# A linear-attention and two-layer MLP kernel on one core: denominators spread by a one-row matmul, float64 weights turned by a scaled copy

## The chip, the core and the metric

The kernel runs on one core of a Trainium2 chip, as one program. The metric is the device time in microseconds. Three runs of the kernel before took 970.0, 970.24 and 970.7 us; the median is 970.24 us.

## The reference, cut to what matters

```python
# q, k, v: (4, 8, 576, 64) float32, w_phi: (64, 128) float32, MLP weights: (512, 2048) and (2048, 512), handed over as float64
def phi(x):
    proj = np.einsum('bhsd,df->bhsf', x, w_phi)
    proj = proj - np.max(np.abs(proj), axis=-1, keepdims=True)
    return np.concatenate([np.exp(proj), np.exp(-proj)], axis=-1)
q_p, k_p = (phi(q), phi(k))
kv = np.einsum('bhsf,bhsd->bhfd', k_p, v)
z = np.sum(k_p, axis=2)
num = np.einsum('bhsf,bhfd->bhsd', q_p, kv)
den = np.einsum('bhsf,bhf->bhs', q_p, z)[..., None] + 1e-06
attn_out = num / den                      # (4, 8, 576, 64) -> x: (2304, 512)

h = x @ w_in;  g = h * (1.0 / (1.0 + np.exp(-h)));  x = g @ w_out              # first layer
h = np.maximum(x @ moe2_w_in, 0.0);  out = (h * h) @ moe2_w_out                 # second layer
```

## The kernel before, in words

The work is cut into eight half blocks of 288 tokens (half a batch each) for the attention, and into six groups of tokens (288, 288, and four times 432) for the first layer. Heads are taken in pairs, p from 0 to 3. `keys_of` makes for each batch and pair the projected keys (`pk`), their exponentials and the product with the values (`pkv`, copied to `kv`). `queries_of(b, p)` does one pair of half block b: the projected queries (`pq`, copied to `qp`), the peak over the features on GpSimd (`qm`), the subtraction on DVE, two exponentials on ScalarE (`qe`), the matmul `pn` with `kv`, which gives 64 rows of numerators and, in row 64, the denominators of 2 x 288 tokens, and a copy of `pn` to the tile `qn` (`num` in the code). For the first batch (b = 0 and 1) these matmuls are float32; later ones are split in a high and a low part.

The denominators stand in one partition. The kernel before spreads them in four steps: a transfer lays the 576 numbers out as 96x6 (`rr`, L1121), DVE adds 1e-6 and takes the reciprocal (L1124, L1125), a second transfer writes them to memory (`rd`, L1128), a third reads them back into 64 partitions (`qb`, L1131). Then DVE multiplies (`x`, L1147), and the product is split in a high part (ScalarE, L431) and a low part (DVE, L435). In the rows `x<-qn,qb` is the product and `x<-x,x` the low part of the split.

The first layer's chunk c of 16 needs the four pairs of its tokens for `h` (L1185) and the weights of chunk c. `h` goes through tanh (ScalarE), a product (DVE, L1193), and a split (`gh` on ScalarE, `gl` on DVE), and then into `o` (L1224). The order number in h_15 is the chunk.

The weights arrive as float64. `w_conv` builds a float32 from the two 32-bit halves: ScalarE takes the magnitude of the upper half (`mag`, L551), and DVE does four steps (`bits`): a clamp (L557), a double shift (L559), an OR with the top bits of the lower half (L563), and an OR with the sign (L567). One call handles 1024 columns in the first layer (16 calls) and 512 in the second (32 calls). `w_split` then makes the high part and the low part (`w<-wc,w`, L435).

The order of the work is not written out by hand. Each step is an `op` with a key, an engine, a cost and buffers; `Plan.run` goes through time with these costs and, whenever an engine is free, takes the ready step with the lowest key whose buffers are free. The order so found is the program's order on each engine, and each engine follows it strictly. The keys come from the table `KEYS`. PSUM has eight banks, parted into pools; `pq` and `pn` of the first half block, like those of the later ones, come from a pool of two banks (`att`).

Of the kernel before, what the change touches and what calls it, by code (L numbers as in the profile page):

```python
# [3 lines left out]

# [5 lines left out]
F32 = mybir.dt.float32  # L10
# [9 lines left out]
NP = H // 2  # L20
# [32 lines left out]
def float_of(bits):
    return struct.unpack("<f", struct.pack("<I", bits))[0]

MIN_HI = float_of(896 << 20)
MAX_HI = float_of((1151 << 20) - 1)

# [227 lines left out]
def dma(kb):  # L288
    return kb
# [11 lines left out]
}  # L301
# [3 lines left out]
def attention_then_two_mlps(ctx, tc, kT, qT, v, w_phi, w1, w2, out):  # L305
# [223 lines left out]
    def w_conv(layer, c, parts, key):  # L529

        n = f"{layer}_{c}_{parts[0]}"
        cols = 512 * len(parts)
        u = plan.unit()
        if layer == 0:
            raw = w_tile("bits", c)
            f = Buf("raw", lambda: rp.tile([128, cols], F32, tag="raw", name="wc" + n), None)
        else:
            raw = Buf("raw", lambda: rp.tile([128, 2 * cols], I32, tag="raw", name="wr" + n), None)  # L540
            f = Buf("c", lambda: cp.tile([128, cols], F32, tag="c", name="wc" + n), None)

        def load():
            src = (w1, w2)[layer][c, :, parts[0] * 512:parts[0] * 512 + cols].bitcast(I32)
            nc.sync.dma_start(out=get(raw), in_=src)

        def halves():
            return get(raw).rearrange("p (n two) -> p n two", two=2)

        def mag():  # L550
            nc.scalar.activation(out=get(f), in_=halves()[:, :, 1].bitcast(F32), func=AF.Abs)  # L551

        def bits(i):
            t, b = get(f), get(f).bitcast(I32)
            lo, hi = halves()[:, :, 0], halves()[:, :, 1]
            if i == 0:
                nc.vector.tensor_scalar(out=t, in0=t, scalar1=MIN_HI, scalar2=MAX_HI, op0=ALU.max, op1=ALU.min)  # L557
            elif i == 1:
                nc.vector.tensor_scalar(  # L559
                    out=b, in0=b, scalar1=5, scalar2=2, op0=ALU.logical_shift_left, op1=ALU.logical_shift_right  # L560
                )
            elif i == 2:
                nc.vector.scalar_tensor_tensor(  # L563
                    out=b, in0=lo, scalar=29, in1=b, op0=ALU.logical_shift_right, op1=ALU.bitwise_or
                )
            else:
                nc.vector.scalar_tensor_tensor(  # L567
                    out=b, in0=hi, scalar=-(1 << 30), in1=b, op0=ALU.bitwise_and, op1=ALU.bitwise_or
                )

        k = ("wf", layer, c, parts[0])
        hold = max([0] + [NC * i + x for i in range(NL) for x in range(NC) if key_of(i, x) <= key - 6]) if layer else 0
        r = [(("c", 0, hold // NC, hold % NC), "h")] if layer else []
        ld = op(key - P["wl"], "SP", dma(cols), load, r=r, w=[(k, 0)], bufs=[raw])
        if layer == 0:
            ld.behind = splits.get(c - NWR)
        op(key, "ACT", act(cols), mag, r=[(k, 0)], w=[(k, 1)], bufs=[raw, f], unit=u)
# [424 lines left out]
    def queries_of(b, p, key, lo_engine="DVE"):  # L1002
# [113 lines left out]
        rb = slot("qb" + n, u, (D, 2, HB))

        rr = Buf("rr", lambda: sp.tile([RP, RN], F32, tag="rr", name="rr" + n), None)

        def spread():  # L1120
            nc.sync.dma_start(out=get(rr), in_=get(num)[D:, :, :].rearrange("p a t -> p (a t)"))  # L1121

        def recip():
            nc.vector.tensor_scalar_add(get(rr), get(rr), 1e-6)  # L1124
            nc.vector.reciprocal(out=get(rr), in_=get(rr))  # L1125

        def r_store():
            nc.sync.dma_start(out=rd[b * NP + p].rearrange("(p f) -> p f", p=RP), in_=get(rr))  # L1128

        def r_load():  # L1130
            nc.sync.dma_start(  # L1131
                out=get(rb).rearrange("p a t -> p (a t)"), in_=rd[b * NP + p].partition_broadcast(D)
            )

        op(key, "SP", dma(3), spread, r=[(Q, "num", 0), (Q, "num", 1)], w=[(Q, "r0")], bufs=[num, rr], unit=u)
        op(key, "DVE", 300, recip, r=[(Q, "r0")], w=[(Q, "r1")], bufs=[rr])
        op(key, "SP", dma(3), r_store, r=[(Q, "r1")], w=[(Q, "r2")], bufs=[rr])
        op(key, "SP", dma(144), r_load, r=[(Q, "r2")], w=[(Q, "r3")], bufs=[rb], unit=u)
        late = b > 0 and p % 2
        x = Buf(  # L1140
            "xy" if late else "xx",
            lambda: (late_pool() if late else sp).tile([128, HB], F32, tag="xx", bufs=1 if late else 2, name="x" + n), None
        )

        def mul():
            for a in range(2):
                nc.vector.tensor_tensor(  # L1147
                    out=get(x)[a * D:(a + 1) * D], in0=get(num)[:D, a, :], in1=get(rb)[:, a, :], op=ALU.mult
                )

        op(key, "DVE", 2 * dve(HB), mul, r=[(Q, "r3"), (Q, "num", 0), (Q, "num", 1)], w=[(Q, "x")],
           bufs=[num, x, rb], unit=u)
        for i, s0, s1 in pieces(b):
            xb = x_buf(i)
            here, there = slice(s0 - b * HB, s1 - b * HB), slice(s0 - STARTS[i], s1 - STARTS[i])

            def x_hi(xb=xb, here=here, there=there):
                hi_act(get(xb)[0][:, p, there], get(x)[:, here])

            def x_lo(xb=xb, here=here, there=there):  # L1160
                lo_on("DVE", get(xb)[1][:, p, there], get(x)[:, here], get(xb)[0][:, p, there])

            op(key, "ACT", act(s1 - s0), x_hi, r=[(Q, "x")], w=[("xh", i, b, p)], bufs=[x, xb])
            op(key, "DVE", dve(s1 - s0), x_lo, r=[(Q, "x"), ("xh", i, b, p)], w=[("xl", i, b, p)], bufs=[x, xb])
# [523 lines left out]
```

## Time and profile before

| | us |
|---|---|
| median of three runs | 970.24 |
| profiled execution | 969.21 |
| span of the profiled execution, first to last instruction | 967.4 |
| TensorE busy | 946.9 |
| VectorE busy | 752.2 |
| ScalarE busy | 613.8 |
| GpSimd busy | 155.8 |

The busy times are of the whole span. An engine that is not the bottleneck may stand idle without cost, and a share of the whole says little about a stage; the stages stand in the rows below. PE is TensorE, DVE is VectorE, ACT is ScalarE, POOL is GpSimd, SP is the engine that issues most transfers. A float32 matmul of the first batch shows as two records.

### The profile page before, as it was taken

The numbers are of one execution on the slowest core, as the hardware profiler recorded it, in microseconds if no ns is written. First come the engines' busy times: TensorE is split into PE (matmuls) and PEld (weight loads), VectorE is DVE, ScalarE is ACT, GpSimd is POOL, SyncE is SP. The second block draws the span as 40 slices with busy tenths as digits, with TensorE's granted clock in tenths as the row PEclk, the third lists the DMA queues.
The fourth block names the chain that finished last, engine by engine and source line by source line (L and its number), as shares of the span: only waits on it lengthen the run. The fifth ranks groups of instructions, "written<-read, shape, count | busy, mean of one in ns | idle before, by whom it ended". The sixth has DMA issues, their size and how long they took to land.

```text
span 967.4 us, 17669 instructions
## 1 busy us (share of the span) xinstructions
PE 946.9 (98%) x6464; PEld 915.0 (95%) x6464; DVE 752.2 (78%) x1362; ACT 613.8 (63%) x1418; POOL 155.8 (16%) x132
## 2 busy tenths in 40 slices
PE   9969999999999999999999999999999999999998
PEld 7749989999999999999999999999999999999998
DVE  6999999777559867889766867885647899898851
ACT  6868877778678887876434444766657765444421
POOL 3140012200042000321000313233110440000000
PEclk9989999999999999999999999999999999999999
DMA  8538645354224654567567575665437774444431
GB/s 315 200 139 324 209 153 172 124 186 136 84 88 132 209 168 136 169 179 253 186 211 263 191 263 166 217 225 217 147 115 237 219 233 121 142 153 134 139 93 51
DMA packets 82322, 171.76 MB, mean 178 GB/s; under 512 B 14906, under 2 KB 39610, under 8 KB 75578
## 3 DMA queue, kind: packets, MB, share of 16 engines
q1 hardware_dynamic: 82234, 170.63, 53.2%
q8 instruction: 51, 0.84, 0.4%
q14 instruction: 37, 0.30, 0.1%
HBM read 123.77 MB, written 46.75 MB: 176 GB/s over the span
## 4 chain that ended last, share of the span: by engine, by line
PE 89%; DVE 7%; ACT 2%; issue 1%; DMA 0%; DVEq 0%; ACTq 0%
PE o L1224 20%; PE h L1185 20%; PE y L1513 17%; PE pb L1341 7%; PE pc L1341 5%; PE pa L1341 5%; PE pn L1106 4%; PE pkv L907 3%; PE pk L845 3%; PE pkv L953 2%; DVE w L435 2%; DVE wc L567 1%; PE pq L1043 1%; PE pq L1044 1%; DVE x L1147 1%
## 5 line engine op out<-in xcount | busy, mean ns | idle before, releaser
L1185 PE MATMUL h<-x,w 128*128 128x432 f32 (+1 forms) x1152 | 217.2, 338 | 2.3 <-DVE x L435 1.7
L1224 PE MATMUL o<-gh,w 128*128 128x432 f32 (+1 forms) x768 | 215.7, 339 | 0.0
L1185 PEld LDWEIGHTS h<-x,w 128*128 128x128 f32 x1152 | 196.8, 188 | 9.4 <-DVE x L435 2.1
L1224 PEld LDWEIGHTS o<-gh,w 128*128 128x128 f32 x768 | 139.8, 188 | 3.9
L1224 PE MATMUL o<-gl,w 128*128 128x432 f32 (+1 forms) x384 | 130.2, 339 | 1.6 <-DVE gl L435 1.4
L1054 POOL PARTITION_ALL_REDUCE qm<-qp x32 | 76.0, 2392 | 261.4 <-ACT qp L1047 236.0
L1189 ACT ACTIVATE a<-h 128x432 f32<-128x432 f32 (+1 forms) x96 | 47.8, 499 | 75.4 <-PE h L1185 75.1
L678 POOL TENSOR_TENSOR ws<-ws 128x256 f32<-128x256 f32 x56 | 52.9, 946 | 198.9 <-DVE wl L435 85.3
L1193 DVE SCALAR_TENSOR_TENSOR a<-a,h 128x432 f32<-128x432 f32 (+1 forms) x96 | 52.7, 550 | 39.2 <-ACT a L1189 38.7
L1224 PEld LDWEIGHTS o<-gl,w 128*128 128x128 f32 x384 | 72.2, 188 | 4.2 <-DVE gl L435 2.5
L435 DVE TENSOR_TENSOR gl<-a,gh 128x432 fp32r<-128x432 f32 (+1 forms) x96 | 57.5, 600 | 14.7 <-ACT gh L431 13.7
L431 ACT CAST gh<-a 128x432 fp32r<-128x432 f32 (+1 forms) x96 | 50.0, 522 | 20.8 <-DVE a L1193 20.3
L1072 ACT ACTIVATE qe<-qp 128x576 f32<-128x576 f32 x64 | 42.1, 683 | 9.3 <-DVE qp L1060 8.4
L879 ACT ACTIVATE ke<-pk,mx 112x128 f32<-112x128 f32 (+1 forms) x160 | 44.5, 376 | 1.0 <-DVE x L1147 0.5
L1513 PE MATMUL y<-yb,w 128*128 128x256 f32 x316 | 44.7, 282 | 0.0
L1106 PE MATMUL pn<-qh,kv 128*65 128x288 f32 x192 | 41.8, 294 | 0.0
L1513 PEld LDWEIGHTS y<-yb,w 128*128 128x128 f32 x316 | 40.7, 189 | 0.0
L435 DVE TENSOR_TENSOR qo<-qe,qh 128x576 fp32r<-128x576 f32 x48 | 36.8, 773 | 4.6 <-ACT qh L431 3.9
L850 DVE TENSOR_REDUCE mx<-pk 112x4 f32<-112x512 f32 (+1 forms) x48 | 28.5, 598 | 14.4 <-PE pk L845 14.1
L953 PEld LDWEIGHTS pkv<-v,kp 112*128 112x128 f32 (+1 forms) x320 | 36.7, 192 | 0.3
L1356 DVE TENSOR_TENSOR glq<-pb,aq 128x288 f32<-128x288 f32 x32 | 14.6, 455 | 28.7 <-PE pb L1341 28.7
L953 PE MATMUL pkv<-v,kp 112*128 112x128 f32 (+1 forms) x320 | 36.9, 275 | 0.0
(425 smaller groups left out, 2601.5 us busy)
## 6 DMA issues: line engine op xcount, KB each, us to landing
w<-w1d SPq DMA_DIRECT2D x30, 1024.0 KB, 5.4
wbits<-w SPq DMA_DIRECT2D x16, 1024.0 KB, 5.9
wr<-w SPq DMA_DIRECT2D x32, 512.0 KB, 5.2
fold<-gd SPq DMA_DIRECT2D x32, 512.0 KB, 3.7
w2d<-wc SPq DMA_DIRECT2D x32, 256.0 KB, 4.1
qr<-qT SPq DMA_DIRECT2D x56, 144.0 KB, 3.4
ws<-w2d SPq DMA_DIRECT2D x28, 256.0 KB, 5.7
w1d<-w SPq DMA_DIRECT2D x6, 1024.0 KB, 4.5
```

Source lines behind the costliest of these rows:

```text
L431: nc.scalar.copy(out=dst, in_=src)
L435: e.tensor_tensor(out=dst, in0=src, in1=hi.bitcast(F32), op=ALU.subtract)
L678: nc.gpsimd.tensor_tensor(out=get(f)[:, o], in0=get(f)[:, a], in1=get(f)[:, b], op=how)
L953: nc.tensor.matmul(get(ps)[:, o:o + 128], get(kps[2 * g + s])[:nt, 2 * i + a], get(vt)[:nt, c:c + 128], start=t == 0 and a == 0 and s == 0 ...
L1054: nc.gpsimd.partition_all_reduce(get(mx), get(pr).rearrange("p a t -> p (a t)"), 128, bass.bass_isa.ReduceOp.absmax)
L1106: nc.tensor.matmul(get(ps)[:D1, :HB], w, get(e)[:, t], start=x == 0, stop=x == len(ops) - 1)
L1185: nc.tensor.matmul(get(ps)[:, :cols], a, x[:, cc, :cols], start=k == 0, stop=k == 3 * ND - 1)
L1189: nc.scalar.activation(out=get(gb)[0][:, :cols], in_=get(ps)[:, :cols], func=AF.Tanh, scale=0.5)
L1193: nc.vector.scalar_tensor_tensor(out=a, in0=a, scalar=1.0, in1=get(ps)[:, :cols], op0=ALU.add, op1=ALU.mult)
L1224: nc.tensor.matmul(get(acc)[:, :cols], a, g[:, :cols], start=c == 0 and x == 0, stop=c == NC - 1 and x == 2)
L1341: nc.tensor.matmul(get(ps)[:, :HB], ws[a][:, f], x[y][:, cc], start=first and k == 0, stop=k == 5, skip_group_check=True,)
L1513: nc.tensor.matmul(get(acc)[:, d * 256:d * 256 + half], get(ws[a][0])[:, ws[a][1], s], both(y)[:, j], start=q == 0 and d == 0 and x == 0, ...
```

## The change

There are two parts, and a new table of keys.

The first: for the first half block (b = 0, four head pairs) DVE adds 1e-6 and takes the reciprocal in place, on the one partition of `qn` that holds the denominators (1x576). Two matmuls with one row of ones as the weights (`ones_row`, set once) spread them over 64 partitions of two PSUM banks (`pr`), and DVE multiplies the numerators with these, one half after the other. The three transfers stay for the later half blocks.

The second: the upper half of a float64 is multiplied on ScalarE with 2^-112, which lowers the exponent as wanted, and the clamp goes. DVE has three steps in place of four: a shift to the left by three with a mask, and the two ORs.

The table of keys has eight other numbers, so that the planner orders many steps in another way.

```diff
-    "k0s": 13.54, "q0s": 16.25, "q0": 5.97, "w0": 42.81, "ws": 4.4, "we": 0.61, "Q1": -4.1, "A1": -0.68,
+    "k0s": 13.54, "q0s": 16.5, "q0": 5.97, "w0": 43.52, "ws": 4.4, "we": 0.61, "Q1": -4.1, "A1": -0.68,
...
+    ones_row = const.tile([D1, D], F32, name="ones_row")
...
+        nc.vector.memset(ones_row[D:], 1.0)
...
         def mag():
-            nc.scalar.activation(out=get(f), in_=halves()[:, :, 1].bitcast(F32), func=AF.Abs)
+            nc.scalar.activation(out=get(f), in_=halves()[:, :, 1].bitcast(F32), func=AF.Copy, scale=2.0 ** -112)
 
         def bits(i):
-            t, b = get(f), get(f).bitcast(I32)
-            lo, hi = halves()[:, :, 0], halves()[:, :, 1]
+            b, lo, hi = get(f).bitcast(I32), halves()[:, :, 0], halves()[:, :, 1]
             if i == 0:
-                nc.vector.tensor_scalar(out=t, in0=t, scalar1=MIN_HI, scalar2=MAX_HI, op0=ALU.max, op1=ALU.min)
+                nc.vector.tensor_scalar(
+                    out=b, in0=b, scalar1=3, scalar2=0x7FFFFFFF, op0=ALU.logical_shift_left, op1=ALU.bitwise_and
+                )
             elif i == 1:
-                nc.vector.tensor_scalar(
-                    out=b, in0=b, scalar1=5, scalar2=2, op0=ALU.logical_shift_left, op1=ALU.logical_shift_right
-                )
-            elif i == 2:
                 nc.vector.scalar_tensor_tensor(
                     out=b, in0=lo, scalar=29, in1=b, op0=ALU.logical_shift_right, op1=ALU.bitwise_or
                 )
             else:
                 nc.vector.scalar_tensor_tensor(
-                    out=b, in0=hi, scalar=-(1 << 30), in1=b, op0=ALU.bitwise_and, op1=ALU.bitwise_or
+                    out=b, in0=hi, scalar=-(1 << 31), in1=b, op0=ALU.bitwise_and, op1=ALU.bitwise_or
                 )
...
-        for i in range(4):
-            op(key, "DVE", dve(cols, i < 2), lambda i=i: bits(i), r=[(k, 1 + i)], w=[(k, 2 + i) if i < 3 else k],
+        for i in range(3):
+            op(key, "DVE", dve(cols, i < 1), lambda i=i: bits(i), r=[(k, 1 + i)], w=[(k, 2 + i) if i < 2 else k],
...
+        row = b < 1
+        if row:
+            def invert():
+                nc.vector.tensor_scalar_add(get(num)[D:], get(num)[D:], 1e-6)
+                nc.vector.reciprocal(out=get(num)[D:], in_=get(num)[D:])
+
+            op(key, "DVE", 1050, invert, r=[(Q, "num", 0), (Q, "num", 1)], w=[(Q, "r2")], bufs=[num], unit=u)
+            over = [bank(f"pr{n}_{a}", u) for a in range(2)]
+            for a in range(2):
+                def copies(a=a):
+                    nc.tensor.matmul(get(over[a])[:D, :HB], ones_row[D:], get(num)[D:, a, :], start=True, stop=True)
...
+        def mul(a):
+            by = get(over[a])[:D, :HB] if row else get(rb)[:, a, :]
+            nc.vector.tensor_tensor(out=get(x)[a * D:(a + 1) * D], in0=get(num)[:D, a, :], in1=by, op=ALU.mult)
```

DVE's order at the place where the first denominators are ready, before: `mx` belongs to the keys of pair 3, `wc` and `w` to the weights of chunks 0 and 1.

```order
L557 TENSOR_SCALAR wc_1_0_371<-wc_1_0_371 128x1024
L559 TENSOR_SCALAR wc_1_0_371<-wc_1_0_371 128x1024
L850 TENSOR_REDUCE mx_3_0_390<-pk_3_0_373 112x4
L435 TENSOR_TENSOR w_0_0_380<-wc_0_0_332,w_0_0_380 128x2x512
L563 SCALAR_TENSOR_TENSOR wc_1_0_371<-wbits_0_162,wc_1_0_371 128x1024
L850 TENSOR_REDUCE mx_3_1_415<-pk_3_1_400 112x4
L850 TENSOR_REDUCE mx_3_2_426<-pk_3_2_409 128x2
L567 SCALAR_TENSOR_TENSOR wc_1_0_371<-wbits_0_162,wc_1_0_371 128x1024
```

The same place after (the line numbers are those of the changed kernel): `qn_0` and `qn_1` are the pairs' tiles, `pr` the spread reciprocals, `x_0` and `x_1` the products.

```order
L549 TENSOR_SCALAR wc_1_0_372<-wc_1_0_372 128x1024
L1109 TENSOR_SCALAR qn_0_377<-qn_0_377 1x576
L1110 RECIPROCAL qn_0_377<-qn_0_377 1x576
L426 TENSOR_TENSOR w_0_0_381<-wc_0_0_334,w_0_0_381 128x2x512
L840 TENSOR_REDUCE mx_3_0_402<-pk_3_0_374 112x4
L1109 TENSOR_SCALAR qn_1_396<-qn_1_396 1x576
L1110 RECIPROCAL qn_1_396<-qn_1_396 1x576
L1151 TENSOR_TENSOR x_0_415<-qn_0_377,pr_0_0_406 64x288
L840 TENSOR_REDUCE mx_3_1_420<-pk_3_1_398 112x4
L1151 TENSOR_TENSOR x_0_415<-qn_0_377,pr_0_1_413 64x288
L1151 TENSOR_TENSOR x_1_432<-qn_1_396,pr_1_0_427 64x288
```

One weight step has gone, and two additions, two reciprocals and four products stand in front of the weights of chunk 1.

PE's order in front of the first h, before: `pn` of the second half block's last pairs, then `h` of chunks 0 to 2 and the keys `pk` of the next batch.

```order
L1106 MATMUL pn_3_0_694<-qe_3_0_676,kv_3_537 65x288
L1106 MATMUL pn_3_0_694<-qe_3_1_684,kv_3_537 65x288
L1106 MATMUL pn_3_1_707<-qe_3_0_676,kv_3_537 65x288
L1106 MATMUL pn_3_1_707<-qe_3_1_684,kv_3_537 65x288
L1185 MATMUL h_0_735<-x_648,w_0_0_380 128x288 x12
L1185 MATMUL h_1_759<-x_648,w_1_0_437 128x288 x12
L845 MATMUL pk_3_0_788<-wbl,kr_3_725 112x256 x2
```

The same place after.

```order
L1096 MATMUL pn_0_1_638<-qe_0_0_612,kv_0_309 65x288
L1096 MATMUL pn_0_1_638<-qe_0_1_616,kv_0_309 65x288
L1030 MATMUL pq_3_0_651<-qr_3_215,wbl 128x288
L1030 MATMUL pq_3_1_656<-qr_3_215,wbl 128x288
L1194 MATMUL h_0_663<-x_446,w_0_0_381 128x288 x12
L835 MATMUL pk_3_0_686<-wbl,kr_3_630 112x256 x2
L1096 MATMUL pn_1_0_695<-qe_1_0_676,kv_1_364 65x288
L1096 MATMUL pn_1_0_695<-qe_1_1_680,kv_1_364 65x288
L1194 MATMUL h_1_705<-x_446,w_1_0_494 128x288 x12
```

Before, all four pairs' `pn` of the second half block stand ahead of the first `h`; after, only pair 0's do, and those of pairs 1 to 3 follow between the first chunks.

## Rows read from the trace of the kernel before

**Rows 1.** The page, busy time of each engine: us (share of the span) xinstructions.

```profile
PE 946.9 (98%) x6464; PEld 915.0 (95%) x6464; DVE 752.2 (78%) x1362; ACT 613.8 (63%) x1418; POOL 155.8 (16%) x132
```

**Rows 2.** Stages: us, PE, PEld, DVE, ACT, POOL busy (instructions), PEclk, DMA share, GB/s.

```profile
48.00:72.00 24.00, 16.04 (x61) 9.55 (x60) 22.84 (x36) 15.90 (x33) 10.73 (x4) 0.86 0.39 136
72.00:96.00 24.00, 23.75 (x174) 22.79 (x172) 23.79 (x44) 21.17 (x63) 0.24 (x2) 1.00 0.90 327
...
300.00:400.00 100.00, 100.00 (x616) 96.44 (x615) 81.12 (x142) 79.77 (x209) 11.96 (x9) 1.00 0.53 171
```

**Rows 3.** What PE waited for, 0 to 150 us: us, times, longest.

```profile
PE pn L1106 <- ACT qe L1072: 5.8, 1, 5.8
...
PE h L1185 <- DVE x L435: 1.7, 2, 0.8
PE o L1224 <- DVE gl L435: 1.4, 2, 1.1
```

**Rows 4.** PE in order of time: start, us, what, idle before it.

```profile
27.46 2.10 PE L1106 MATMUL pn<-qe,kv 128*65 128x288 f32 x8
29.40 1.46 PE L845 MATMUL pk<-wbl,kr 128*112 128x256 f32 x6
...
31.67 9.10 PE L953 MATMUL pkv<-v,kp 112*128 112x128 f32 x80
...
55.67 10.83 PE L1106 MATMUL pn<-qe,kv 128*65 128x288 f32 x32 [5.81 <-ACT qe L1072]
...
70.49 2.12 PE L1185 MATMUL h<-x,w 128*128 128x288 f32 x14 [0.85 <-DVE x L435]
...
144.47 3.42 PE L1185 MATMUL h<-x,w 128*128 128x288 f32 x24 [0.17 <-DVE w L435]
```

**Rows 5.** DVE in order of time: start, us, what.

```profile
42.68 0.68 DVE L557 TENSOR_SCALAR wc<-wc 128x1024 f32<-128x1024 f32 x1
43.28 1.21 DVE L563 SCALAR_TENSOR_TENSOR wc<-wbits,wc 128x1024 int32<-128x1024 int32 x1
44.42 0.68 DVE L559 TENSOR_SCALAR wc<-wc 128x1024 int32<-128x1024 int32 x1
...
47.90 1.21 DVE L435 TENSOR_TENSOR w<-wc,w 128x1024 fp32r<-128x1024 f32 x1
49.03 1.21 DVE L567 SCALAR_TENSOR_TENSOR wc<-wbits,wc 128x1024 int32<-128x1024 int32 x1
...
61.91 0.75 DVE L1060 TENSOR_TENSOR qp<-qp,qm 128x576 f32<-128x576 f32 x1
62.58 1.22 DVE L563 SCALAR_TENSOR_TENSOR wc<-wbits,wc 128x1024 int32<-128x1024 int32 x1
...
69.98 0.45 DVE L435 TENSOR_TENSOR x<-x,x 128x288 fp32r<-128x288 f32 x1
70.35 1.22 DVE L563 SCALAR_TENSOR_TENSOR wc<-wbits,wc 128x1024 int32<-128x1024 int32 x1
...
145.38 1.60 DVE L435 TENSOR_TENSOR qo<-qe,qh 128x576 fp32r<-128x576 f32 x2
```

**Rows 6.** The tile rr on DVE: durations in ns, min/median/max, first and last start.

```profile
L1124 DVE TENSOR_SCALAR rr<-rr x32: 125/161/1285, 40.9 to 474.1; 96x6 f32<-96x6 f32 x32
L1125 DVE RECIPROCAL rr<-rr x32: 186/186/189, 41.1 to 474.3; 96x6 f32<-96x6 f32 x32
```

**Rows 7.** DVE's groups by line and shape: busy us, mean ns, idle before.

```profile
L435 DVE TENSOR_TENSOR ql<-qr,ql 64x576 fp32r<-64x576 f32 x24 | 18.0, 755 | 4.9 <-ACT ql L431 4.3
...
L557 DVE TENSOR_SCALAR wc<-wc 128x512 f32<-128x512 f32 x32 | 14.6, 457 | 3.9 <-ACT wc L551 3.8
...
L856 DVE TENSOR_TENSOR kd<-pk,mx 112x512 f32<-112x512 f32 x6 | 4.1, 687 | 0.1
...
L496 DVE TENSOR_TENSOR wbl_lo<-wbl,wst_hi 64x128 fp32r<-64x128 f32 x2 | 0.6, 279 | 0.0
```

More of the change, by code (lines that the diff above doesn't have):

```diff
@@ L1 @@
 import heapq
-import struct
 from contextlib import ExitStack
@@ L50, in key_of @@
     return NC * STARTS[i] / HB + c * WIDTHS[i] / HB
[L53 to L59, printed above, removed]
 class Op:
@@ L1114, in queries_of @@
             op(key, "ACT", act(HB, True), evac, r=[(Q, "n", a)], w=[(Q, "num", a)], bufs=[ps, num], unit=u)
[L1116 to L1137, printed above, removed]
@@ L1138, in queries_of, with spread, recip, r_store @@
-        op(key, "SP", dma(144), r_load, r=[(Q, "r2")], w=[(Q, "r3")], bufs=[rb], unit=u)
+        row = b < 1
[8 more added lines that the diff above has]
+                    nc.tensor.matmul(get(over[a])[:D, :HB], ones_row[D:], get(num)[D:, a, :], start=True, stop=True)
+                op(key, "PE", 4 * MM, copies, r=[(Q, "r2"), "blank"], w=[(Q, "r3", a)], bufs=[num, over[a]], unit=u)
+        else:
+            rb = slot("qb" + n, u, (D, 2, HB))
+            rr = Buf("rr", lambda: sp.tile([RP, RN], F32, tag="rr", name="rr" + n), None)
+            def spread():
+                nc.sync.dma_start(out=get(rr), in_=get(num)[D:, :, :].rearrange("p a t -> p (a t)"))
+            def recip():
+                nc.vector.tensor_scalar_add(get(rr), get(rr), 1e-6)
+                nc.vector.reciprocal(out=get(rr), in_=get(rr))
+            def r_store():
+                nc.sync.dma_start(out=rd[b * NP + p].rearrange("(p f) -> p f", p=RP), in_=get(rr))
+            def r_load():
+                nc.sync.dma_start(
+                    out=get(rb).rearrange("p a t -> p (a t)"), in_=rd[b * NP + p].partition_broadcast(D)
+                )
+            op(key, "SP", dma(3), spread, r=[(Q, "num", 0), (Q, "num", 1)], w=[(Q, "r0")], bufs=[num, rr], unit=u)
+            op(key, "DVE", 300, recip, r=[(Q, "r0")], w=[(Q, "r1")], bufs=[rr])
+            op(key, "SP", dma(3), r_store, r=[(Q, "r1")], w=[(Q, "r2")], bufs=[rr])
+            op(key, "SP", dma(144), r_load, r=[(Q, "r2")], w=[(Q, "r3")], bufs=[rb], unit=u)
@@ L1143, in queries_of @@
         )
-        def mul():
+        def mul(a):
+            by = get(over[a])[:D, :HB] if row else get(rb)[:, a, :]
+            nc.vector.tensor_tensor(out=get(x)[a * D:(a + 1) * D], in0=get(num)[:D, a, :], in1=by, op=ALU.mult)
+        if row:
             for a in range(2):
[L1147 to L1152, printed above, removed]
+                op(key, "DVE", dve(HB), lambda a=a: mul(a), r=[(Q, "r3", a), (Q, "num", a)], w=[(Q, "x", a)],
+                   bufs=[num, x, over[a]], unit=u)
+            got = [(Q, "x", 0), (Q, "x", 1)]
+        else:
+            op(key, "DVE", 2 * dve(HB), lambda: [mul(a) for a in range(2)],
+               r=[(Q, "r3"), (Q, "num", 0), (Q, "num", 1)], w=[(Q, "x")], bufs=[num, x, rb], unit=u)
+            got = [(Q, "x")]
         for i, s0, s1 in pieces(b):
@@ L1161, in x_lo @@
                 lo_on("DVE", get(xb)[1][:, p, there], get(x)[:, here], get(xb)[0][:, p, there])
-            op(key, "ACT", act(s1 - s0), x_hi, r=[(Q, "x")], w=[("xh", i, b, p)], bufs=[x, xb])
-            op(key, "DVE", dve(s1 - s0), x_lo, r=[(Q, "x"), ("xh", i, b, p)], w=[("xl", i, b, p)], bufs=[x, xb])
+            op(key, "ACT", act(s1 - s0), x_hi, r=got, w=[("xh", i, b, p)], bufs=[x, xb])
+            op(key, "DVE", dve(s1 - s0), x_lo, r=[*got, ("xh", i, b, p)], w=[("xl", i, b, p)], bufs=[x, xb])
     accs = {}
```

4 rows, old and new, of the table KEYS are left out of this document.

## The prediction

> **What bounds the kernel now.** I read the page first, then the stages, then what TensorE waits for, then the two engines' rows in order of time. The page shows TensorE (PE) busy 946.9 of 967.4 us and VectorE (DVE) 752.2 [rows 1]. The stages show where the missing 20 us lie: from 200 us on PE is full (100.00 of 100.00 from 300 to 400, DVE 81.12), but from 48 to 72 us it is busy only 16.04 of 24 and its granted clock falls to 0.86, while DVE is busy 22.84 [rows 2]. So one stage has another limit than the rest: at the start DVE is the bound, later PE is. The list of PE's waits agrees: its longest is 5.8 us in front of pn, and most others end on DVE's x or gl [rows 3]. The rows of that stage show why: PE stands before 55.67, does 16 pn matmuls (32 records, two to a float32 matmul) in 10.83 us, and gets the last part of the first h only at 70.49 [rows 4]. That part waits for DVE's x<-x, which starts at 69.98 and ends at about 70.35 [rows 5]. This last x is the event to follow: the numerators of head pair 3 pass through the adding of 1e-6, the reciprocal, three transfers, the product and the split, all threaded through a full DVE queue.
>
> **The change part by part.** The sum is made against the profiled execution, 969.21 us with a span of 967.4; the median of the runs shown is 970.24, so I add 1.0 at the end.
>
> *DVE up to the last x.* I count the instructions that stand ahead of the last x in DVE's order, before and after, and price them by the distance from one start to the next in a full queue [rows 5]: a tensor_scalar on 1024 columns 0.60 us (42.68 to 43.28), a scalar_tensor_tensor 1.14 (43.28 to 44.42), a split of w 1.13 (47.90 to 49.03), a qp subtraction 0.67 (61.91 to 62.58). Before, 14 such tensor_scalars stand ahead of it, after, 5: -5.4 us. Two scalar_tensor_tensors, two splits and three subtractions move behind it: -2.3, -2.3 and -2.0. Six small pairs on rr go from in front of it: 0.161 and 0.186 us less some overlap, 0.29 a pair, -1.7 [rows 6]. Four tensor_scalars on 1x576 come in. The 96x6 one takes 161 ns and one on 1024 columns 0.68 us [rows 5, 6], so 576 columns take 0.45, less 0.08 of overlap (0.68 long, but the next starts after 0.60): 0.37 each, +1.5. Without the reciprocals this is -12.2 us. The eight half products stay eight; that they read PSUM now costs nothing that I can see, since subtractions that read pk take 687 ns for 512 columns, no more than other rows of that width [rows 7].
>
> *The four reciprocals on one partition.* The trace has reciprocals on 6 columns only: 186 ns [rows 6]. Plain two-input rows take 279 ns at 128 columns and 687 at 512 [rows 7], a slope of 1.06 ns and 143 ns at no columns. Two readings bound the price. If the reciprocal streams like every other row of the trace and has only a longer start, 576 columns take 186 + 570 x 1.06 = 790 ns, less overlap 0.71 us. If all 43 ns above 143 are its six elements, it is 7.2 ns an element and, with the fixed part of a full queue, 4.2 us. I take 0.71, since no other DVE row of this trace streams at more than about 1.06 ns when undisturbed, and a constant of 37 ns explains 186 as well; I keep 4.2 for the range. The Trainium skill (VectorE: DVE Perf Modes, section First, the fixed hardware budget) says that the reciprocal is an iterated divide with a repeat count of eight. Eight passes of 1.04 ns would give an estimate of 4.8 us; no run here shows a long reciprocal, and the 6-column row lies between the two. With 0.71 the four add 2.8: DVE reaches the last x 12.2 - 2.8 = 9.4 us earlier, at 60.9.
>
> *PE up to the first h.* Eight one-row matmuls are new. No row shows one with a single row of weights; a float32 matmul of the same 288 columns takes 0.485 us (27.46 to 29.40 for four) [rows 4], so eight cost 3.9; from below they could cost nothing, if one row were free, but then no streamed column cost anything, so I take 3.9. From 30.4 us to the end of the first h PE then has 40 pkv at 0.223 (80 records in 9.10, less the drain), 30 matmuls at 0.485, one pk and 12 h at 0.13 [rows 4]: 25.5 us. That fits into the 31 us to 61.3, so the 3.9 us lie in what was idle time, and DVE still sets the first h. PE's instructions run in order, so a late reciprocal would hold up pq and pkv behind it; at 0.71 us that is a us or two.
>
> *PE from the first h to the last h of the first half block (h_15).* Before, the first h ends at about 70.9 and h_15 at 147.9 (144.47 plus 3.42) [rows 4]: 77.0 us, nearly all busy, with 1.9 us of waits. After, 12 pn matmuls of the second half block stand behind the first h instead of ahead (5.8 us) and 8 single-pass pq come forward (1.05): 83.9 us. From 61.3 that is 145.2, 2.7 earlier, and the 1.05 is work done ahead of time: 3.7 us in all.
>
> *Does DVE hold that pace?* From the last x to the last split of w before h_15 DVE took 75.0 us (70.35 to 145.38) [rows 5]. After: 7 tensor_scalars fewer (-4.2), the two scalar_tensor_tensors, two splits, two qp and two rr pairs that were moved (+2.3, +2.3, +1.3, +0.6), and two ql more at 0.75 (+1.5) [rows 7]: 78.8, which ends at 139.7, and two h of 1.6 behind it at 142.9. So PE is the limit, with 2.3 us in reserve.
>
> *What costs or gives nothing.* The 32 tensor_scalars removed from the second layer's weights (457 ns each [rows 7]) lie in the stage where PE is full and DVE has a fifth of its time free [rows 2]: zero; were that cover gone, they would be 10 us. The Abs that becomes a scaled copy stays one pass of ScalarE over the same columns: zero either way. Twelve transfers leave SyncE's queue; x no longer waits for them, which is the 9.4 already counted. The other shifts of order fall into full PE time; I allow 1 us either way.
>
> Sum: 967.4 - 3.7 = 963.7 span, 965.5 for a profiled execution, **966.5 us** beside the median.
>
> **The rivals.**
> *A, the long reciprocal (slower).* At 3.9 to 4.2 us each the four put 12.8 to 14.0 us more in front of the last x, PE stands at pr_1 and again at pr_3 with pq and pkv queued behind, and the first h ends at 74 or later. The forecast's -3.7 becomes +9 to +10.3: 979 to 980.5. It decides from the point where a reciprocal costs more than 0.71 + 3.7/4 = 1.6 us. For it: the 186 ns beside the 161 of the row before it. Against it: two lengths are not told apart by one size. By the skill's eight passes the same sum is 983 (an estimate). Chance 0.27.
> *B, the gain is used up (no change).* pr takes both PSUM banks that pq and pn share, so pr_1 waits for the products of pair 0 and pq_3 for those of pair 1; DVE and PE then wait for each other in turn, and the reserve of 2.3 us plus the gain of 3.7 is gone when these waits come to 6 us. For it: both engines are busy over 98% from 72 to 96 us [rows 2]. Against it: DVE has other work between the products. 970. Chance 0.17.
> *C, more comes back.* The 1.9 us of waits that I kept vanish, as gl and w come earlier, and the second half block gains too: DVE's 142.9 becomes the end of h_15, -6: 964. Chance 0.14.
>
> **How the numbers follow.** The forecast has 0.42, with 964.5 to 968.5 as its own range. About 0.2% (2 us) is what a measurement of this kernel can tell from no change. Faster: most of the forecast, C and a little of B, 0.53; within: 0.18; slower: A and a rest, 0.29. The range reaches from 963.5 to 980, which leaves out the long end of A and the best of C. The likeliest case's own range is the narrow one.
>
> **What would show it.** The reciprocals on qn under 0.8 us; the last x of the first half block near 61 us; no PE gap of 5 us before 60; the granted clock near 1.00 from 48 to 72; h_15 ending near 145; PE full from 200 on. Wrong, if a reciprocal takes over 1.6 us, if PE stands for more than 2 us in front of a pr, or if PE waits grow between 61 and 145.

## The result and the profile after

The changed kernel takes 977.8 us (median of 4 runs, 976.42 to 978.58), beside 970.12 for the kernel before on the same chip: a ratio of 1.0081, 95% interval 1.0069 to 1.0094. It is 0.8% slower, where 966.5 us had been forecast. The profiled execution has a span of 976.5 us, 9.1 more than before.

The stages of the kernel after (columns as in [rows 2]):

```profile
24.00:48.00 24.00, 18.11 (x88) 12.88 (x87) 22.27 (x23) 15.34 (x41) 2.58 (x3) 0.79 0.30 105
48.00:72.00 24.00, 18.73 (x85) 12.31 (x84) 22.95 (x22) 12.67 (x24) 5.29 (x4) 0.79 0.46 158
...
120.00:148.00 28.00, 28.00 (x224) 27.61 (x224) 27.03 (x38) 21.78 (x57) 0.12 (x1) 1.00 0.55 188
...
800.00:900.00 100.00, 97.46 (x804) 96.86 (x803) 86.84 (x166) 45.88 (x88) 6.07 (x4) 0.98 0.45 136
```

The loss stands at the start. From 24 to 72 us PE is busy only 36.84 of 48 us, at a granted clock of 0.79, between its levels of 1.2 and 2.4 GHz (before, 38.92 us, at 1.00 and 0.86); DVE is busy 45.2 of the 48. From 120 to 148 PE is full, which it was not in the kernel before:

```profile
120.00:148.00 28.00, 26.50 (x198) 25.39 (x198) 27.20 (x35) 20.03 (x43) 4.33 (x2) 1.00 0.50 186
```

A second, small loss is at 800 to 900 (97.46, before 99.42). PE's waits in the kernel after name the step:

```profile
PE pr L1116 <- DVE qn L1110: 11.2, 4, 4.3
```

Four waits, 11.2 us, in front of the one-row matmuls, for line 1110, the reciprocal. This wait is new; that of 5.8 us for qe [rows 3] is gone. The tile qn, in the form of [rows 6], gives the price of each new instruction:

```profile
L1116 PE MATMUL pr<-qn,ones_row x16: 401/551/708, 32.3 to 66.0; 1*64 1x288 f32 x16
L1151 DVE TENSOR_TENSOR x<-qn,pr x8: 446/446/450, 38.3 to 70.3; 64x288 f32<-64x288 f32 x8
L1109 DVE TENSOR_SCALAR qn<-qn x4: 450/452/903, 27.9 to 59.7; 1x576 f32<-1x576 f32 x4
L1110 DVE RECIPROCAL qn<-qn x4: 3744/3744/3745, 28.4 to 60.7; 1x576 f32<-1x576 f32 x4
```

The addition takes the 0.45 us of the forecast, the product from PSUM 446 ns. The reciprocal takes 3744 ns; the forecast had 790. DVE's rows show what follows, as [rows 5] did for before:

```profile
55.59 0.45 DVE L1109 TENSOR_SCALAR qn<-qn 1x576 f32<-1x576 f32 x1 [0.83 <-ACT qn L1099]
56.07 3.74 DVE L1110 RECIPROCAL qn<-qn 1x576 f32<-1x576 f32 x1
59.74 0.90 DVE L1109 TENSOR_SCALAR qn<-qn 1x576 f32<-1x576 f32 x1
60.68 3.75 DVE L1110 RECIPROCAL qn<-qn 1x576 f32<-1x576 f32 x1
...
71.93 1.55 DVE L426 TENSOR_TENSOR x<-x,x 128x288 fp32r<-128x288 f32 x1
```

Two reciprocals fill 7.5 of the 8.4 us from 56 to 64.4. The last x of the first half block ends at 73.5; the forecast had 60.9, and it was 70.35 before. This last x takes 1.55 us, where it took 0.45 before [rows 5]; a reduction on GpSimd runs beside it (71.27 to 74.02), as one does beside the addition of 0.90 us (58.19 to 60.33). Whether that is the reason was not tried. PE's rows, as in [rows 4]:

```profile
38.39 2.15 PE L1116 MATMUL pr<-qn,ones_row 1*64 1x288 f32 x4 [4.34 <-DVE qn L1110]
40.47 2.29 PE L1030 MATMUL pq<-qr,wbl 128*128 128x288 f32 x4
42.55 10.27 PE L943 MATMUL pkv<-v,kp 112*128 112x128 f32 x80
...
56.53 1.62 PE L1030 MATMUL pq<-qr,wbl 128*128 128x288 f32 x6
...
64.57 2.15 PE L1116 MATMUL pr<-qn,ones_row 1*64 1x288 f32 x4 [3.46 <-DVE qn L1110]
66.65 3.25 PE L1030 MATMUL pq<-qr,wbl 128*128 128x288 f32 x6
...
73.68 1.97 PE L1194 MATMUL h<-x,w 128*128 128x288 f32 x12
...
152.97 6.53 PE L1194 MATMUL h<-x,w 128*128 128x288 f32 x48
```

PE takes its instructions in order, so pq and pkv stand behind each pr. After the waits of 4.34 and 3.46 us they also run slower: six pq records take 3.25 us at 66.65, where six took 1.62 at 56.53. The granted clock of the kernel after, in stretches of 4 us (columns as in [rows 2]), shows why:

```profile
36.00:40.00 4.00, 1.61 (x4) 0.73 (x4) 3.91 (x5) 1.07 (x5) 0.00 (x0) 0.50 0.00 0
40.00:44.00 4.00, 4.00 (x13) 2.96 (x12) 3.94 (x8) 3.84 (x16) 0.00 (x0) 0.50 0.37 100
...
64.00:68.00 4.00, 3.43 (x7) 1.81 (x8) 3.91 (x7) 1.38 (x2) 0.00 (x0) 0.50 0.26 45
68.00:72.00 4.00, 4.00 (x9) 2.19 (x9) 3.94 (x5) 3.65 (x8) 3.04 (x2) 0.50 0.99 380
```

A granted clock of 0.50 is the level of 1.2 GHz; in the kernel before one such stretch (56 to 60) has it, behind the wait of 5.8 us. The page of the kernel after has PE's busy time of the whole span:

```profile
PE 955.0 (98%) x6480; PEld 920.9 (94%) x6480; DVE 742.6 (76%) x1315; ACT 613.0 (63%) x1418; POOL 153.7 (16%) x132
```

So PE stands idle for 21.5 us (976.5 - 955.0), hardly longer than the 20.5 of before (967.4 - 946.9 [rows 1]). Of the 9.1 us of span 8.1 are busy time: 16 records of pr are new, and matmuls behind the two long waits run at the lower clock.

The last row of PE holds h_14, h_15 and two chunks of the next group; its first half, up to h_15, ends at 156.2, which was 147.9 before. So 8.3 of the 9.1 us of span are lost by then.

### The profile page after: what moved, and what is told of

The parts are those of the page before. It is cut to its first block, busy times and chain, and to the rows that moved or that the text cites. A ratio compares the mean times of both kernels' runs of the same rounds, so it can differ in the third digit from the quotient of the medians.

```text
span 976.5 us, 17633 instructions
## 1 busy us (share of the span) xinstructions
PE 955.0 (98%) x6480; PEld 920.9 (94%) x6480; DVE 742.6 (76%) x1315; ACT 613.0 (63%) x1418; POOL 153.7 (16%) x132
## 4 chain that ended last, share of the span: by engine, by line
PE 94%; DVE 4%; issue 1%; ACT 1%; POOL 1%; POOLq 0%; DVEq 0%
PE o L1233 21%; PE h L1194 21%; PE y L1522 17%; PE pb L1350 7%; PE pa L1350 5%; PE pc L1350 5%; PE pn L1096 5%; PE pkv L943 4%; PE pk L835 3%; PE pkv L897 3%; DVE qn L1110 1%; PE pq L1030 1%; PE pq L1033 1%; PE pq L1034 1%; DVE w L426 1%
## 5 line engine op out<-in xcount | busy, mean ns | idle before, releaser
L1044 POOL PARTITION_ALL_REDUCE qm<-qp x32 | 72.9, 2298 | 237.9 <-ACT qp L1037 225.9
L1198 ACT ACTIVATE a<-h 128x432 f32<-128x432 f32 (+1 forms) x96 | 47.3, 494 | 61.3 <-PE h L1194 60.6
L840 DVE TENSOR_REDUCE mx<-pk 112x4 f32<-112x512 f32 (+1 forms) x48 | 28.5, 597 | 16.5 <-PE pk L835 16.3
L422 ACT CAST w<-ws 128x512 fp32r<-128x512 f32 (+2 forms) x36 | 24.0, 687 | 18.1 <-POOL ws L668 14.4
```

Of the source, the lines that this page charges most:

```text
L422: nc.scalar.copy(out=dst, in_=src)
L1044: nc.gpsimd.partition_all_reduce(get(mx), get(pr).rearrange("p a t -> p (a t)"), 128, bass.bass_isa.ReduceOp.absmax)
L1198: nc.scalar.activation(out=get(gb)[0][:, :cols], in_=get(ps)[:, :cols], func=AF.Tanh, scale=0.5)
```

## The experiments

Theory L: the length of the reciprocal alone, 3.0 us more than forecast and four times in front of the last x, is the cause. Its rivals: turn-taking of the engines over two PSUM banks (T), the new keys (K), the weights' part (W).

### The reciprocal replaced by an operation that streams (e4)

```diff
-                nc.vector.reciprocal(out=get(num)[D:], in_=get(num)[D:])
+                nc.vector.tensor_tensor(
+                    out=get(num)[D:], in0=get(num)[D:], in1=ones_row[D:, :1].unsqueeze(2).to_broadcast([1, 2, HB]), op=ALU.min
+                )
```

> The changed kernel with one instruction replaced, four times: the reciprocal of 1x576 becomes a two-input minimum of 1x576, so the division by the denominators is left out. Every other instruction, its place in each engine's order and each wait stay. Theory L (the length of the reciprocal is the cause: 3.74 us each, at 3.0 us more than the forecast had): the minimum takes about 0.75 us, the last x of the first half block ends near 61 to 62 us instead of 73.4, PE stands no 4 us in front of a pr, and the kernel takes 965 to 968 us, about 0.2 to 0.5% less than the kernel before. Rival T (two PSUM banks and turn-taking of the two engines, or the one-row matmuls themselves, are the cause): the waits in front of pr stay and the time stays at 975 to 978. Rival K (the new order after the first h is worse): last x near 61, but PE's waits between 61 and 145 us grow and the time is 970 or more.

Measured: 964.03 us (five runs from 961.61, the profiled one, to 965.0), ratio 0.9934 (0.9921 to 0.9947): 13.8 us less than the changed kernel, from four instructions. Rows of DVE and then PE, with PE's waits:

```profile
49.92 0.75 DVE L1110 TENSOR_TENSOR qn<-qn,ones_row 1x576 f32<-1x576 f32 x1
...
59.95 0.45 DVE L426 TENSOR_TENSOR x<-x,x 128x288 fp32r<-128x288 f32 x1
```

```profile
50.06 2.15 PE L1118 MATMUL pr<-qn,ones_row 1*64 1x288 f32 x8
...
60.46 0.53 PE L1196 MATMUL h<-x,w 128*128 128x288 f32 x2 [0.62 <-DVE x L426]
...
139.11 6.53 PE L1196 MATMUL h<-x,w 128*128 128x288 f32 x48
```

```profile
PE warm L512 <- ACT zeros L477: 2.3, 1, 2.3
PE pn L1096 <- ACT qe L1062: 1.9, 2, 1.4
PE y L1524 <- DVE yd_3l L426: 0.9, 1, 0.9
```

The page of its profile:

```profile
PE 948.0 (99%) x6480; PEld 916.4 (95%) x6480; DVE 734.3 (77%) x1315; ACT 611.4 (64%) x1418; POOL 152.6 (16%) x132
```

No wait in front of pr is left. At its forecast price the step does what the forecast said: last x at 60.4 (forecast 60.9), first h at 61.0 (61.3), h_15 at 139.11 + 6.53/2 = 142.4 (145.2). T and K fall: banks, one-row matmuls and keys are all still there. L came out 1 us better than its range. The spans of the two profiled executions differ by 16.7 us (976.5 and 959.8). PE's idle time makes 9.7 of this (21.5 against 11.8), and 7.0 is a longer busy time for the same 6480 matmul records; no stretch of 4 us up to 72 us lies below a granted clock of 0.71 here. So the reciprocal costs in two ways: PE waits for it, and then runs slower. Without the division x holds other numbers, but twelve h take 1.97 us in both kernels.

### Half of the reciprocal (e8)

```diff
-                nc.vector.reciprocal(out=get(num)[D:], in_=get(num)[D:])
+                nc.vector.reciprocal(out=get(num)[D:, 0, :], in_=get(num)[D:, 0, :])
+                nc.vector.tensor_tensor(
+                    out=get(num)[D:, 1, :], in0=get(num)[D:, 1, :], in1=ones_row[D:, :1].to_broadcast([1, HB]), op=ALU.min
+                )
```

> A dose: the changed kernel, but only the first 288 of a pair's 576 denominators get the reciprocal, the other 288 the two-input minimum (so half of the division is left out). Order of all other instructions as in the changed kernel. Theory L (6.24 ns a column, the length of the reciprocal in front of the last x sets the loss): the reciprocal of 1x288 takes 186 + 282 x 6.24 = 1.95 us; with the minimum behind it, about 2.3 us stand where the streaming version has 0.7 and the changed kernel 3.7, so 53% of the way: the last x ends near 67.3 us and the kernel takes about 971 (970 to 973). Rival P (a long instruction of fixed length, whatever its columns): 3.7 us or more for 288 columns and 978 or more. Rival T (a threshold: PE's slack hides a reciprocal up to some length): no more than 966.

Measured: 969.94 us, ratio 1.0001 (0.9992 to 1.0009). DVE's rows:

```profile
56.83 1.94 DVE L1110 RECIPROCAL qn<-qn 1x288 f32<-1x288 f32 x1
58.70 0.39 DVE L1111 TENSOR_TENSOR qn<-qn,ones_row 1x288 f32<-1x288 f32 x1
...
67.75 0.45 DVE L426 TENSOR_TENSOR x<-x,x 128x288 fp32r<-128x288 f32 x1
```

The 1.94 us answer to 6.24 ns a column; P falls, and so does the threshold of T. The last x ends at 68.2, and the time lies a hair under L's range: of 13.8 us between no reciprocal and the whole, this half costs 5.9 and the other 7.9. With 2.3 us for a pair the change is worth nothing: with this table of keys, this is the measured point of balance.

### The price of a reciprocal by its size (e10)

```diff
+        for rows in (1, 64, 128):
+            for cols in (6, 32, 64, 128, 256):
+                for _ in range(2):
+                    nc.vector.reciprocal(out=flat[:rows, :cols], in_=flat[:rows, :cols])
```

> The changed kernel with thirty reciprocals added behind its end (1, 64 and 128 partitions by 6, 32, 64, 128 and 256 columns, each twice); only their durations are read, the time is longer by what they take. Theory L: 149 ns and 6.24 ns for each column, whatever the partitions: about 186, 350, 550, 950 and 1745 ns in all three rows of partitions. Rival O (one partition is what makes it slow): 64 and 128 partitions take 1.06 ns a column, about 190, 215, 250, 320 and 455 ns. Rival S (eight passes of 1.04 ns): 8.3 ns a column, about 2200 ns for 256.

The groups of DVE by line and shape (busy us, mean ns):

```profile
L1659 DVE RECIPROCAL wbl<-wbl 128x256 f32<-128x256 f32 x2 | 3.5, 1753 | 0.1
L1659 DVE RECIPROCAL wbl<-wbl 64x256 f32<-64x256 f32 x2 | 3.5, 1745 | 0.1
L1659 DVE RECIPROCAL wbl<-wbl 1x256 f32<-1x256 f32 x2 | 3.5, 1741 | 0.1
...
L1659 DVE RECIPROCAL wbl<-wbl 128x64 f32<-128x64 f32 x2 | 1.1, 552 | 0.1
...
L1659 DVE RECIPROCAL wbl<-wbl 1x64 f32<-1x64 f32 x2 | 1.1, 542 | 0.1
...
L1659 DVE RECIPROCAL wbl<-wbl 1x6 f32<-1x6 f32 x2 | 0.4, 179 | 0.1
```

From 6 to 256 columns on one partition: (1741 - 179)/250 = 6.25 ns a column; 128 partitions cost 12 ns more in all. So one partition is not slow as such; 576 columns in a row are. In the form 96x6 of the kernel before the same 576 numbers take 186 ns [rows 6].

### The parts one by one, with the keys as they were

Four kernels take one part alone, or one part away. The weights' part alone in the kernel before (e1, the edit of `mag` and `bits` in the change's diff):

> The kernel before with the weights' part of the change alone: scaled copy on ScalarE, three steps on DVE, the three transfers and the keys of before. Theory L: this part was priced rightly (a tensor_scalar on 1024 columns is worth 0.60 us of a full DVE queue); some 6 fewer stand ahead of the last x, so it ends about 3 us earlier (near 67), if the transfers of the denominators do not come to be late instead; 966 to 968.5 us, 0.2 to 0.4% less than before. Rival W (the weights' part costs, because the order that the planner finds is worse or the transfers bind): 970 or more.

The changed kernel without the weights' part (e2, the same edit reversed):

> The changed kernel with the weights' part undone: Abs, clamp and two shifts, four steps on DVE, the new keys, the one-row matmuls and the long reciprocals stay. Theory L: the four reciprocals put about 12 us more in front of the last x than the forecast had, and the nine tensor_scalars of that stretch come back with 0.6 us each, so the last x ends near 78 to 79 us and the kernel takes 979 to 983, slower than the changed kernel. Rival W (the weights' part is what made the changed kernel slow): 970 or less.

The kernel before with the new keys (e3) and the changed kernel with the old ones (e5):

```diff
-    "k0s": 13.54, "q0s": 16.25, "q0": 5.97, "w0": 42.81, ...
+    "k0s": 13.54, "q0s": 16.5, "q0": 5.97, "w0": 43.52, ...
```

> The kernel before with the new table of keys alone. Theory L: 969 to 972, no difference that can be measured. Rival K (the new order is the cause): 974 to 978.

> The changed kernel with the keys of before. Up to the last x DVE's order is that of the changed kernel, so the last x ends at 73.4 again. Theory L with the keys fitted to each set of steps: the loss of the changed kernel stays and the later stages lose besides, 980 to 990 us. Rival K (the new keys made the changed kernel slow): 970 or less.

| | us | ratio to before (95%) |
|---|---|---|
| e1, weights alone | 982.52 | 1.0129 (1.0116 to 1.0143) |
| e2, weights undone | 1001.86 | 1.0330 (1.0316 to 1.0344) |
| e3, keys alone | 982.17 | 1.0128 (1.0114 to 1.0142) |
| e5, keys undone | 982.75 | 1.0135 (1.0117 to 1.0154) |

Only e5 came as expected: its last x ends at 73.0, and PE waits 11.2 us in front of pr, as in the changed kernel. The other three lie 10 to 19 us above what theory L gave, e1 on W's side, e3 even above K's. In e2 the last x ends at 73.4, as in the changed kernel, where 78 to 79 had been expected; in e1 it ends at 69.9, where 67 had been. The stage from 400 to 500 us in e3, its waits there, and the same stage in e2:

```profile
400.00:500.00 100.00, 91.81 (x503) 86.92 (x502) 77.12 (x146) 61.83 (x139) 19.03 (x8) 0.95 0.46 154
```

```profile
PE pn L1106 <- DVE qo L435: 3.9, 2, 3.4
PE pn L1106 <- ACT qh L431: 2.2, 1, 2.2
```

```profile
400.00:500.00 100.00, 91.33 (x524) 83.98 (x523) 79.89 (x148) 69.80 (x169) 17.93 (x9) 0.95 0.46 152
```

This is far from the change: the queries of the last half block come too late for their pn, 100.00 of 100 in before and after becomes 91 to 92, and the clock falls to 0.95 besides. In e1 PE loses less at a time: at 200 to 300 (97.83) it waits 1.3 us for the keys' low part kl, at 600 to 700 (96.70) 2.0 and 0.9 us for gh and gl. Each table does better with the steps it belongs to than the other table does. So the order is a part of each kernel that can't be held fixed while a step is taken away: the time lost when one part is undone is not the worth of that part. K falls as the cause (the old keys make the changed kernel slower still, 982.75); W stays open with e1 as it is.

### The weights' part with a table of its own (e12)

```diff
-    "Q2": 17.0, "Q3": 19.0, "A2": 29.74, "Q4": 42.0, "Q5": 61.0, "A3": 60.97, "Q6": 66.0, "Q7": 91.57,
+    "Q2": 17.0, "Q3": 19.0, "A2": 28.52, "Q4": 42.0, "Q5": 60.15, "A3": 62.12, "Q6": 66.0, "Q7": 91.57,
...
-    "qs": 0.24, "ks": -0.73, "w2a": 66.58, "w2b": 2.2, ...
+    "qs": 0.43, "ks": -0.73, "w2a": 63.54, "w2b": 2.1, ...
```

> The weights' part alone again (as in e1: the kernel before with the scaled copy and three steps), but with a table of keys fitted by the planner to this set of steps; the transfers of the denominators stay. Ahead of the last x stand 7 tensor_scalars fewer than in the kernel before and one scalar_tensor_tensor more: -4.2 + 1.1 = -3.1 us. Theory F (a part is worth what it was priced at once the table of keys belongs to it; e1 lost 12 us because its keys belonged to another kernel): last x near 67, no stretch after 200 us with PE under 98, 965 to 968.5 us. Rival W (the three steps or the scaled copy themselves cost): 975 or more, as e1. Rival D (the transfers bind once DVE is earlier): last x stays at 70 or later and the time at 969 to 971.

Measured: 966.05 us, ratio 0.9958 (0.9944 to 0.9971). This version beats both kernels. The stage from 120 to 148 us, and the last x:

```profile
120.00:148.00 28.00, 28.00 (x219) 28.00 (x218) 25.40 (x35) 19.87 (x42) 9.19 (x4) 1.00 0.50 176
```

```profile
69.56 0.45 DVE L435 TENSOR_TENSOR x<-x,x 128x288 fp32r<-128x288 f32 x1
```

Theory F and D are each half right. The last x ends at 70.0, hardly earlier than the 70.35 of before, as D said. That the transfers of the denominators or the exponentials (PE waits 7.7 us for qe) hold it there was not tried. But the time is F's, though 700 to 800, at 97.90, lies a hair under F's 98. Behind its last wait for qe, which ends at 62.17, PE waits for nothing up to 200 us, where before it waited 1.7 us for x and 1.4 for gl [rows 3]; this fits DVE's fewer steps, but is not shown to come from them. W falls: with a table of its own the weights' part does not cost, and the keys alone make 16.5 us between e1 and this version. The 3.7 us less than before are the part and its new table together, since the kernel before with another search of its table was not tried.

### The reciprocal made short, in two ways

By two transfers in place of three (e6): the denominators go to 96x6, are inverted there, and come back to the row for the one-row matmul.

```diff
+            def spread():
+                nc.sync.dma_start(out=get(rr), in_=get(num)[D:, :, :].rearrange("p a t -> p (a t)"))
...
+            def back():
+                nc.sync.dma_start(out=get(num)[D:, :, :].rearrange("p a t -> p (a t)"), in_=get(rr))
```

> The changed kernel with the short reciprocal of before: a transfer lays the denominators out as 96x6, DVE adds and inverts there, a second transfer brings them back to the row, and the one-row matmul spreads them. Theory L: the two small steps cost DVE 0.3 us a pair in place of 4.2, no 4-us wait of PE in front of a pr; the transfers (about 2 us each to land) lie beside other work of DVE. 964 to 970. Rival K (the planner's order for this set of steps): 972 to 985.

Measured: 975.65 us, ratio 1.0067 (1.0054 to 1.0079); rival K's range. The last x ends at 68.4, and PE no longer stands 4 us in front of a pr, but it waits 5.1 us for qh in the last half block and is busy 94.57 of 100 from 400 to 500. A table fitted to this version was not tried.

By PE (e7, and e13 with a table of its own):

```diff
+                for c in range(12):
+                    nc.tensor.matmul(
+                        get(over[0])[:48, c:c + 1], den[:, 48 * c:48 * c + 48], ones_row[D:, :1], start=True, stop=True
+                    )
...
+                nc.vector.tensor_scalar_add(rc, get(over[0])[:48, :12], 1e-6)
+                nc.vector.reciprocal(out=rc, in_=rc)
+                nc.vector.tensor_tensor(
+                    out=get(dg)[:48].rearrange("i a (c j) -> i (a c) j", j=48),
+                    in0=ident[:48, :48].unsqueeze(1).to_broadcast([48, 12, 48]),
+                    in1=rc.unsqueeze(2).to_broadcast([48, 12, 48]), op=ALU.mult
+                )
```

> A version that keeps the matmul in place of the transfers and makes the reciprocal short: twelve one-column matmuls turn the 576 denominators to 48x12 in PSUM, DVE adds 1e-6, takes the reciprocal of 12 columns and multiplies it into a diagonal (48x576), and a matmul with 48 rows of ones spreads each half over 64 partitions; the identity is made at the start. Theory L: DVE spends about 0.17 + 0.22 + 0.75 = 1.1 us a pair, as little as the streaming version (1.2), so the last x ends between 60 and 65 us and the kernel takes 963 to 968, faster than both. Rival K (the keys are fitted to another set of steps, and the planner's order for this one loses what the steps gain): 972 to 985. Rival T (turn-taking of DVE and PE over two banks, now with one more turn for each pair): waits of PE in front of the one-column matmuls and of pr of over 1 us each, 970 or more.

> The version of e7 (denominators turned to 48x12 by one-column matmuls, short reciprocal, diagonal, matmul with ones) with a table of keys fitted by the planner to it. Ahead of the last x stand one tensor_scalar, two scalar_tensor_tensors and one split of w more than in the streaming version (0.60 + 2.3 + 1.1 = 4.0 us), so the last x ends near 64. Theory F: no loss of PE between 400 and 500 us, 963 to 967 us, faster than both kernels. Rival T (one more turn between the engines for each pair): 970 or more.

Measured: e7 973.55 us, ratio 1.0047 (1.0033 to 1.0061); e13 969.79, ratio 1.0000 (0.9992 to 1.0009). Rival K was right for e7 (95.61 from 400 to 500); its last x, at 68.8, also missed the 60 to 65 that L gave. With its own table that loss is gone, and the last x ends at 65.2 as expected near 64; but 963 to 967 was missed. Two stages of e13, and its PE rows in the first:

```profile
24.00:48.00 24.00, 24.00 (x158) 17.82 (x158) 19.30 (x29) 17.36 (x44) 2.08 (x3) 0.86 0.48 180
...
600.00:700.00 100.00, 96.03 (x710) 94.69 (x710) 76.45 (x147) 64.07 (x148) 26.40 (x24) 1.00 0.59 208
```

```profile
33.18 1.29 PE L1121 MATMUL pr<-ones_row,qn 1*48 1x1 f32 x24
...
37.65 6.34 PE L949 MATMUL pkv<-v,kp 112*128 112x128 f32 x40
...
45.13 4.63 PE L949 MATMUL pkv<-v,kp 112*128 112x128 f32 x40
```

PE has no idle time from 24 to 48 us, and yet its clock is granted at 0.86: 40 pkv behind the second group of one-column matmuls take 6.34 us, the next 40 take 4.63. That the one-column matmuls lower the clock is not shown: in e7 they stand in this stage too, at a granted clock of 1.00 (0.86 in the next), and the streaming version has 0.93 without them. More is lost at 600 to 700, where pb, a matmul of the second layer, waits 1.4 and 1.7 us for the high and low parts that DVE splits off. T's waits are small (1.2 us for dg in all). Why e13 ends at 969.8 with its last x at 65.2, where the half reciprocal ends at 969.9 with 68.2, is not settled; the stage from 600 to 700, which is full in the half version, is one part of it.

### The planner told the true length (e14)

```diff
-            op(key, "DVE", 1050, invert, r=[(Q, "num", 0), (Q, "num", 1)], w=[(Q, "r2")], bufs=[num], unit=u)
+            op(key, "DVE", 4200, invert, r=[(Q, "num", 0), (Q, "num", 1)], w=[(Q, "r2")], bufs=[num], unit=u)
```

> The changed kernel where the planner is told the measured length of the addition and the reciprocal (4.2 us in place of 1.05), with a table of keys fitted to that. Theory L (the time of DVE itself is spent, whoever knows of it): the planner can put 6 steps of the weights behind the last x, which then ends near 69, but the weights come later by the same amount; 972 to 980 us, not faster than the kernel before. Rival M (only the planner's wrong figure did the harm, an order made for the true one gets the gain): 968 or less.

Measured: 975.26 us, ratio 1.0059 (1.0047 to 1.0072), in L's range; M falls. The last x comes at 67.1, but PE's clock from 48 to 72 is 0.72, and PE is busy 25.88 of 28 from 120 to 148, where it waits 1.3 us for gl and 0.8 for gh. The four reciprocals take 3.74 us of DVE each in this order too. An early last x alone does not make the kernel fast: here it ends 1.1 us before that of the half reciprocal, and the time is 5.3 us longer.

## Why the prediction was wrong, point by point

**The step that failed: "The four reciprocals on one partition", where I took 0.71 us.** Measured 3744 ns; in the queue one fills 3.67 us (56.07 to 59.74) and the others 3.77, together 12.1 more than taken. Put into the prediction's own sum, the last x comes at 60.9 + 12.1 = 73.0 (measured 73.5) and -3.7 becomes +8.4, a span of 975.8 (measured 976.5). That this comes so near is in part luck: the first h ends at 75.6, where the mended sum has 73.4, and from there to h_15 it is 80.6 us, where the sum has 83.9. Nor has the sum a term for the clock, which fell to 0.50 behind the two long waits. Rival A is what happened, at 0.27; its price of 3.9 to 4.2 us was nearer than the forecast's, and its 979 to 980.5 lies 1.2 us or more above the 977.8. Two of the prediction's signs of being wrong came: a reciprocal over 1.6 us, and PE standing over 2 us in front of a pr. The reason given for 0.71, that no other DVE row streams at more than 1.06 ns a column, was an argument from other operations. The row of 6 columns allowed either reading, and of the two the longer one was nearly right: (3744 - 186)/570 = 6.24 ns a column, beside the 7.2 that the row gave when its fixed part was taken from plain rows. The Trainium skill (VectorE: DVE Perf Modes, First, the fixed hardware budget) names a repeat count of eight; the eight passes estimated from it gave 4.8 us, 28% too much; the trace shows 6.24 ns a column, some six of the plain slope. The estimate pointed to the right side.

**DVE without the reciprocals: right.** -12.2 + 2.8 was tested by the streaming version, 0.75 us for each of the four: the last x at 60.4 against 60.9.

**PE up to the first h: right** in the streaming version (61.0 against 61.3). In the changed kernel the late reciprocal held up pq and pkv, as that step said it would.

**PE and DVE to h_15: too careful.** In the streaming version h_15 ends 5.5 us earlier than before, not 2.7. From the first h to h_15 it takes 81.4 us, where the sum had 83.9; of the 1.9 us of waits that the sum kept, 0.5 is left, and the other 1.1 us were not traced. That was rival C (964, with h_15 at 142.9). The balance lies higher than the 1.6 us a reciprocal that rival A gave: 2.3 us for a pair gave no difference.

**Rival B (two banks, turn-taking): not seen** where the reciprocal is short. **No cost of the PSUM product: right** (446 ns). **The second layer's 32 tensor_scalars at zero: not measured by themselves**; from 600 to 900 PE loses 2.8 us before and 2.2 in the streaming version. **"I allow 1 us" for the other shifts of order:** true of this change, but only as its table was fitted to it; with a table of another kernel the order alone costs 12 us. What makes 97.46 of the changed kernel's 800 to 900 us was not tried apart.

**What the parts are worth.** The weights' part with its own table: 966.05, -3.7 us against before. The row on top of it, at a streaming price: 964.03, 2.0 less. The row with the real reciprocal: 977.8, 11.8 more. The tables differ between these kernels, and a table of another kernel costs 5.0 us (e5 beside the changed kernel) to 16.5 us (e1 beside e12), so these differences hold only as far as each table is well fitted. The reciprocal itself, with the table held, is the 13.8 us of the streaming version.

## What to carry to other kernels

When a row of the trace can be read in two ways that differ fivefold, and the time's sign hangs on it, the row is not evidence for the cheap reading; bound the chance by the row nearest in kind (another reciprocal), not by the many rows of other operations. An operation whose price goes by columns wants its data laid over partitions before it runs, and a transfer that does so may be earning its keep. Where an order is fitted to a set of steps, test a part only with an order fitted again, or change a single instruction and leave the order alone.

## What the runs showed of the hardware

- A float32 reciprocal on DVE takes about 6.25 ns a column, the same on 1, 64 and 128 partitions (1741, 1745 and 1753 ns for 256 columns); a plain two-input row goes by 1.06 [rows 7].
- One-row matmuls (1x64 weights, 288 columns) cost about what full ones do: four of them (8 records) take 2.15 us at 50.06 in the streaming version, and 8 records of pn 2.10 [rows 4].
- Behind waits of 4.34 and 3.46 us TensorE was granted 0.50, its level of 1.2 GHz, from 36 to 44 and from 64 to 72 us; six pq records took 3.25 us there, and 1.62 at 56.53, where the clock was 1.00.
- A TensorE that stands idle nowhere by its records may still be granted less than its full clock: 24.00 of 24 us busy at 0.86 (e13, 24 to 48 us), of which the one-column matmuls are 48 records and 2.52 us. What lowered it there stays open.
